# One yield more ahead of three readers, z loaded once, and a warm-up in half rows: a three-layer kernel on one Trainium2 core

## The chip, the cores and the metric

The kernel runs on one core of a Trainium2 chip. The core has five engines that run their own instruction queues and wait for one another through semaphores: TensorE (PE, matrix products; PEld is its weight load), VectorE (DVE), ScalarE (ACT), GpSimd (POOL) and SyncE (SP). SP, ACT and POOL also issue DMA transfers. The metric is the device time of one execution in microseconds.

## The reference

Two batches of 3136 tokens with 256 features pass through three layers:

```python
scores = (1 / S) * z @ z.T                    # attention, z has 64 features
x = u * (np.maximum(scores, 0) ** 2 @ v)
u1 = x + (x.T @ U @ V).T                      # layer 1: rank-32 token mixing
x = u1 + np.maximum(u1 @ w_ch1, 0) @ w_ch2    # 256 -> 1024 -> 256
u2 = x + real(fft(fft(x, axis=1), axis=2))    # layer 2: Fourier mixing
un = (u2 - mean) / sqrt(var + 1e-6)           # over the features
out = u2 + np.maximum(un @ w_ch1b, 0) @ w_ch2b
```

## The kernel before

**Number format.** Products run in a single-pass float32 format. Each operand is split into a rounded part and a remainder (a cast on ACT in `hcopy`, line 93, and a subtraction on DVE in `sub`, line 96), and a product is the sum of three (high by high, high by low, low by high).

**Attention** (lines 385 to 751) goes by batch, by 7 query chunks of 448 tokens and by 13 pairs of 128 keys. For z the two parts lie on top of each other in one tile of 128 partitions, T1 (high in the lower 64, remainder in the upper 64), and T2 holds them the other way round, so that two products with K = 128 give the scores. `load_z` (395) brings a chunk of z in twice, once for each half of the partitions, `split_z` (401) makes T1 and, for the very first chunk, T2. Lines 659 to 672 are the start of the program: three products of a zeroed tile, then the first loads and splits. The first loads are the only ones that also use ACT's DMA queue.

**Layers 1 and 2** go by 28 chunks of 448 tokens: 14 of layer 1, 14 of layer 2. The order of work is written by hand, from line 980. A chunk has 8 steps; at step k PE makes hidden block k (`hidden`, line 324, six products into one of three psH buffers, then `Hh` on ACT and `Hl` on DVE) and the six products of `project` (339) for the hidden block of two steps before, into psC, which has one buffer for each half of the output. After the last of them `finish` (360) reads psC on DVE; in layer 2 it multiplies by `rs`, one over the standard deviation, spread over 128 partitions (line 377, and 371 in the last chunk), adds x (379) and stores.

Between these products each step advances a list of Python generators by one `yield`; newer ones of the next chunk stand first. What a generator issues up to its next `yield` comes, on every engine, behind the products of that step. Three kinds matter here:

- `prep2` (274) of each layer-2 chunk starts at step 2 of the chunk before. It makes the mean (product of line 284), the centred and split input, the squares, their sum over the features (product of line 302 at step k=1 of the chunk itself), then a row of variances that goes through a small tile by DMA (`vv`, 306), a square root (310), a reciprocal chain (313 to 317), a DMA to DRAM (`rsd`, 319) and a broadcast back (`rs`, 321). The last three stand in step k=5.
- `fourier(b)` (782) adds the Fourier mixing of one batch to x, the first batch during layer 1, the second from step 106, the third step of the first layer-2 chunk. Its `fold` (792, six small additions on DVE) feeds `tokens` (810, transposes on PE) one step later; then come products along one axis (`axis49`), reloads, products along the other (`axis64`, 866), and `features` (887), nine products on PE, then DVE's additions to x. A single feature, number 128, is made apart (`feature128`, 881) and enters `features` as a row that two DMAs on POOL's queue write (line 953), read by the product of line 894.
- `weights`, `prep1` and the conversions, which the change doesn't touch.

POOL's queue holds `vv`, `rsd`, `rs`, the feature row and the reloads of T2, each issued in program order; an issue whose data isn't there yet holds up those behind it.

Of the kernel before, what the change touches and what calls it, by code (L numbers as in the profile page):

```python
# [10 lines left out]
F32 = mybir.dt.float32  # L11
# [10 lines left out]
CH = 448  # L22
# [55 lines left out]
def f(ap):  # L78
    return ap.bitcast(F32)
# [3 lines left out]
def program(ctx, tc, zT, v, uT, U, V, w1a, w2a, w1b, w2b, b49, f64, fd, rep, mask, out):  # L83
# [8 lines left out]
    def hcopy(o, i):  # L92
        nc.scalar.copy(o, i)  # L93

    def sub(o, a, b):
        tt(out=o, in0=a, in1=b, op=ALU.subtract)  # L96
# [10 lines left out]
    def ptile():  # L107
        return ctile("P", bufs=4)
# [114 lines left out]
    class Chunk:  # L223
# [4 lines left out]
        def load(self, a):  # L228
            self.a = a
            load(out=a, in_=aT_d[self.b][:, :, self.sl].rearrange("a p n -> p a n"))  # L230
            self.vr = com.tile([128, CH], F32, tag="Vr", name="Vr", bufs=1)
            for k in range(4):
                load(out=self.vr[k * 32 : k * 32 + 32, :], in_=V_d[:, self.sl])
# [40 lines left out]
        def prep2(self):  # L274
            b, mp = self.b, late["mp"]
            x = late["xT"][b][:, :, self.sl]
            h, l = c2(ctile("h", F32R)), c2(ctile("l", F32R))
            s = self.halved(x)
            yield
            st = self.stacked(*s)  # L280
            yield
            yield
            mu = misc()
            mm(mu[:, 0:CH], ones, st, start=True, stop=True)
            cc, sq = c2(ptile()), c2(ptile())
            for k in range(2):
                sub(cc[:, k], x[:, k], mu[:, 0:CH])
            yield
            for k in range(2):
                hcopy(h[:, k], x[:, k])  # L290
                sub(l[:, k], x[:, k], f(h[:, k]))
            self.x, self.h, self.l = x, h, l
            yield
            for k in range(2):
                act(out=sq[:, k], in_=cc[:, k], func=AF.Square)
            s = self.halved(sq)
            yield
            st = self.stacked(*s)
            yield

            ps = misc()
            mm(ps[0:1, 0:CH], ones[:, 0:1], st, start=True, stop=True)
            row = mp.tile([1, CH], F32, tag="vrow", name="vrow", bufs=1)
            hcopy(row, ps[0:1, 0:CH])
            vv, y, r0, ve = (mp.tile([112, 4], F32, tag=t, name=t) for t in ("vv", "vy", "vr", "ve"))
            late_dma(out=vv, in_=row.rearrange("o (p j) -> o p j", j=4))
            yield
            yield
            yield
            act(out=y, in_=vv, func=AF.Sqrt, bias=maskc[0:112, 3:4])  # L310
            nc.vector.tensor_scalar_add(ve, vv, 1e-6)
            yield
            nc.vector.reciprocal(r0, y)
            tt(out=y, in0=r0, in1=r0, op=ALU.mult)
            tt(out=y, in0=y, in1=ve, op=ALU.mult)
            nc.vector.tensor_scalar(out=y, in0=y, scalar1=-0.5, scalar2=1.5, op0=ALU.mult, op1=ALU.add)
            tt(out=y, in0=y, in1=r0, op=ALU.mult)
            row_d = rs_d[b * NC + self.c]
            late_dma(out=row_d.rearrange("(p j) -> p j", j=4), in_=y)
            self.rs = mp.tile([128, CH], F32, tag="rs", name="rs")  # L320
            late_dma(out=self.rs, in_=row_d.partition_broadcast(128))
            yield
# [62 lines left out]
    def attention(stack):  # L385
# [7 lines left out]
        Uhl = att.tile([128, 25, 2, RANK], F32R, tag="U", name="Uhl", bufs=1)  # L393

        def load_z(b, c):
            raw = att.tile([128, CH], F32, tag="zraw", name="zraw")
            for h, dma in enumerate((load, nc.scalar.dma_start if (b, c) == (0, 0) else load)):
                dma(out=raw[h * 64 : h * 64 + 64, :], in_=zT[b, :, c * CH : c * CH + CH])
            zraw[b, c] = raw

        def split_z(b, c):
            raw = zraw.pop((b, c))
            if c == 0:
                T1[b] = big.tile([128, S], F32R, tag="T1", name=f"T1_{b}")
            dst = T1[b][:, c * CH : c * CH + CH]
            hcopy(dst, raw)
            if (b, c) == (0, 0):
                t = T2[0, 0] = att.tile([128, CH], F32R, tag="T2", name="T2")
                hcopy(t[64:128], raw[64:128])
                sub(dst[64:128], raw[64:128], f(dst[64:128]))  # L410
                sub(t[0:64], raw[0:64], f(dst[0:64]))
            else:
                sub(dst[64:128], raw[64:128], f(dst[64:128]))
            if c == NC - 1:
                T1d[b] = att.tile([128, 2, 64], F32R, tag="T1d", name=f"T1d_{b}")
                for h in range(2):
                    nc.vector.tensor_copy(T1d[b][:, h, :], f(T1[b][:, S - 64 : S]))
# [238 lines left out]
        jobs = conversions()  # L656


        t = ptile()
        nc.vector.memset(t[:, 0:352], 0.0)  # L660
        hcopy(t[:, CH : CH + 8], t[:, 0:8])
        ps = pmg.tile([128, 512], F32, tag="g", name="ps_g")
        for k in range(3):
            mm(ps[:, 0:352], t[:, 0:128], t[:, 0:352], start=True, stop=True)
        load_z(0, 0)
        load_v(0, 0)
        load_z(0, 1)
        load_v(0, 1)
        split_z(0, 0)
# [112 lines left out]
    def fourier(b):  # L782
# [64 lines left out]
        for i in range(10):  # L847
            if i < 8:
                fold(i)
            if 0 < i < 9:  # L850
                tokens(i - 1)
            if i == 7:
                load(out=raw128[0:32, :], in_=xT[b][0:1, 1, :].rearrange("o (s p) -> o s p", p=98))
            if i > 1:
                axis49(i - 2)
            yield
# [82 lines left out]
        for pairs in (range(0, 3), range(3, 6), range(6, 9), range(9, 13)):  # L939
            first = 2 * pairs[0]  # L940
            k = min(2 * pairs[-1] + 2, KPOS) - first
            Th, Tl = (mp.tile([128, 2, CH], F32R, tag=t, name=t, bufs=1) for t in ("Th", "Tl"))
            for g in pairs:
                axis64(g, first, Th, Tl)
                if g + 3 < 13:
                    fetch(g + 3)
                if g == 1:
                    feature128()
                if g == pairs[-1]:

                    row = rows[pairs[0] // 3 % 2]
                    for j, x in enumerate((ch, cl)):
                        nc.gpsimd.dma_start(
                            out=row[j : j + 1, 0 : k * 64].rearrange("o (k n) -> o k n", n=64),
                            in_=x[first : first + k, :],
                        )
                if late_adds is not None and next(late_adds, "end") == "end":
                    late_adds = None
                yield
            yield  # L960
            late_adds = features(first, k * 64, Th, Tl, row)
            next(late_adds)
            yield
# [94 lines left out]
```

## Time and profile before

| | us |
|---|---|
| three runs: median (lowest, highest) | 1218.28 (1218.10, 1219.21) |
| the profiled execution | 1218.11 |
| its span, first to last instruction | 1216.3 |
| PE busy | 1202.9 |
| DVE busy | 829.8 |
| ACT busy | 652.5 |
| POOL busy | 46.8 |
| share of PE in the chain that ended last | 90% |

The span is what the profiler saw from the first instruction to the last; the profiled execution's time has 1.8 us around it. Busy times are unions, with matmuls shown longer than their distance, so PE can be called busy across short waits. A wait is read from the idle time in front of an instruction and from what ended it; the loss is read from the distance of starts.

### The profile page before, as it was taken

Reading aid. Unit: us, or ns where it says so; the run is one execution under the profiler, and the core shown is the slowest. Engines: PE = TensorE matmul, PEld = TensorE weight load, DVE = VectorE, ACT = ScalarE, POOL = GpSimd, SP = SyncE. Lnnn points to the kernel's source line nnn. Section 1 sums busy time; section 2 is a strip of 40 time slices with the busy share of each in tenths; the row PEclk is TensorE's granted clock in tenths of the full one; section 3 lists DMA queues with packets and bytes.
Section 4 is the critical chain, followed back from the end, with each engine's and each line's share of the span. In section 5 each row is a group of like instructions: output and inputs, shape, how many; then the busy total and the mean of one; then the engine's idle time right before and its main releaser. Section 6 shows DMA issues by size and latency. Waiting matters only on the chain.

```text
span 1216.3 us, 16363 instructions
## 1 busy us (share of the span) xinstructions
PE 1202.9 (99%) x6038; PEld 1102.4 (91%) x6038; DVE 829.8 (68%) x1565; ACT 652.5 (54%) x1052; POOL 46.8 (4%) x94
## 2 busy tenths in 40 slices
PE   9999999999999999999999999999999999999998
PEld 7999999999999999999899998999989889999997
DVE  7867777888666667666555456476576688666664
ACT  7767667777666566665433334333255444444442
POOL 0000000000000000000000000000000101000100
PEclk9999999999999999999999999999999999999999
DMA  5302220333122012211111102212012111111111
GB/s 153 104 22 69 68 64 26 117 93 105 44 64 64 9 57 77 60 40 54 38 51 53 46 23 85 81 45 62 5 57 73 48 39 31 39 31 38 31 39 46
DMA packets 58688, 68.56 MB, mean 56 GB/s; under 512 B 11630, under 2 KB 53712, under 8 KB 58608
## 3 DMA queue, kind: packets, MB, share of 16 engines
q1 hardware_dynamic: 54144, 61.13, 16.4%
q0 software_dynamic: 4384, 6.27, 2.6%
q8 instruction: 47, 0.77, 0.3%
q14 instruction: 33, 0.27, 0.1%
q10 hardware_dynamic: 80, 0.11, 0.0%
HBM read 44.86 MB, written 19.56 MB: 53 GB/s over the span
## 4 chain that ended last, share of the span: by engine, by line
PE 90%; DVE 4%; issue 3%; DMA 1%; ACT 1%; POOL 0%; SPq 0%; DVEq 0%; POOLq 0%; ACTq 0%
PE psO L574 12%; PE psO L571 12%; PE psO L573 11%; PE psH L330 6%; PE psH L329 6%; PE psH L331 6%; PE psC L355 6%; PE psC L354 6%; PE psC L356 6%; PE psS L542 6%; PE psS L541 6%; PE ps_g L628 1%; PE ps_m L607 1%; DVE Hl L335 1%; DVE l L96 0%
## 5 line engine op out<-in xcount | busy, mean ns | idle before, releaser
L571 PE MATMUL psO<-h,Vt 128*128 128x448 f32 x700 | 256.6, 367 | 0.1
L574 PE MATMUL psO<-h,Vt 128*128 128x448 f32 x700 | 256.5, 366 | 0.0
L573 PE MATMUL psO<-l,Vt 128*128 128x448 f32 x672 | 246.3, 367 | 0.3 <-DVE l L96 0.2
L547 ACT ACTIVATE P<-psS 128x896 f32<-128x896 f32 (+1 forms) x183 | 161.6, 884 | 147.7 <-PE psS L542 147.2
L335 DVE SCALAR_TENSOR_TENSOR Hl<-psH,Hh 128x448 fp32r<-128x448 f32 x224 | 139.6, 623 | 142.7 <-ACT Hh L334 141.6
L334 ACT ACTIVATE Hh<-psH 128x448 fp32r<-128x448 f32 x224 | 121.8, 544 | 200.2 <-PE psH L331 197.1
L96 DVE TENSOR_TENSOR l<-P,h 128x896 fp32r<-128x896 f32 (+1 forms) x197 | 201.2, 1021 | 23.5 <-ACT h L93 17.7
L551 DVE CAST h<-P 128x896 fp32r<-128x896 f32 (+1 forms) x183 | 111.0, 606 | 145.7 <-ACT P L550 144.6
L550 ACT ACTIVATE P<-P 128x896 f32<-128x896 f32 (+1 forms) x183 | 168.4, 921 | 5.7
L329 PE MATMUL psH<-h,w 128*128 128x448 f32 x448 | 167.9, 375 | 0.0
L330 PE MATMUL psH<-l,w 128*128 128x448 f32 x448 | 164.5, 367 | 0.2 <-DVE l L96 0.2
L331 PE MATMUL psH<-h,w 128*128 128x448 f32 x448 | 164.5, 367 | 0.0
L355 PE MATMUL psC<-Hl,w 128*128 128x448 f32 x448 | 163.7, 365 | 0.0
L354 PE MATMUL psC<-Hh,w 128*128 128x448 f32 x448 | 163.7, 365 | 0.0
L356 PE MATMUL psC<-Hh,w 128*128 128x448 f32 x448 | 163.2, 364 | 0.0
L571 PEld LDWEIGHTS psO<-h,Vt 128*128 128x128 f32 x700 | 131.6, 188 | 11.4 <-DVE aT L586 0.6
L574 PEld LDWEIGHTS psO<-h,Vt 128*128 128x128 f32 x700 | 131.6, 188 | 11.2 <-DVE Vt L96 0.3
L573 PEld LDWEIGHTS psO<-l,Vt 128*128 128x128 f32 x672 | 126.4, 188 | 11.3 <-DVE l L96 0.9
L541 PE MATMUL psS<-T 128*128 128x448 f32 x336 | 125.2, 373 | 0.8 <-DVE T L96 0.8
L542 PE MATMUL psS<-T,T 128*128 128x448 f32 x336 | 124.2, 370 | 0.0
L329 PEld LDWEIGHTS psH<-h,w 128*128 128x128 f32 x448 | 84.7, 189 | 7.9 <-ACT h L93 0.3
L331 PEld LDWEIGHTS psH<-h,w 128*128 128x128 f32 x448 | 84.4, 188 | 7.3
(276 smaller groups left out, 1421.8 us busy)
## 6 DMA issues: line engine op xcount, KB each, us to landing
uT<-in_uT SPq DMA_DIRECT2D x14, 448.0 KB, 4.2
vraw<-in_v SPq DMA_DIRECT2D x24, 256.0 KB, 2.7
out<-P SPq DMA_DIRECT2D x27, 224.0 KB, 2.0
aTd<-aT SPq DMA_DIRECT2D x13, 448.0 KB, 3.0
P<-aTd SPq DMA_DIRECT2D x13, 448.0 KB, 3.6
scr<-wst SPq DMA_DIRECT2D x16, 256.0 KB, 2.0
Vr<-Vd SPq DMA_DIRECT2D x56, 56.0 KB, 3.0
rs<-rsd POOLq DMA_DIRECT2D x14, 224.0 KB, 3.6
```

The source lines that it names most:

```text
L96: tt(out=o, in0=a, in1=b, op=ALU.subtract)
L329: mm(ps[:, 0:CH], wh, self.h[:, a], start=a == 0, stop=False)
L330: mm(ps[:, 0:CH], wh, self.l[:, a], start=False, stop=False)
L331: mm(ps[:, 0:CH], wl, self.h[:, a], start=False, stop=a == 1)
L354: mm(dst, wh, h, start=k == 0, stop=False)
L355: mm(dst, wh, l, start=False, stop=False)
L356: mm(dst, wl, h, start=False, stop=k == 7)
L541: mm(ps[:, j, 0:CH], k, q1, start=True, stop=False)
L542: mm(ps[:, j, 0:CH], k, q2, start=False, stop=True)
L571: mm(dst, vh, hj, start=p == 0 and j == 0, stop=False)
L573: mm(dst, vh, lj, start=False, stop=False)
L574: mm(dst, vl, hj, start=False, stop=p == 12)
```

## The change

- **Sum product and `rs`:** one more `yield` in `prep2` between the split squares and the product of line 302, and one more between the issues of `rsd` and `rs`.
- **z:** `load_z` loads 64 partitions once; `split_z` casts them into the lower half of T1 and writes the remainder, by a subtraction that reads the lower half, into the upper. T2 of the first chunk is made from the same 64 partitions.
- **Warm-up:** the zeroed tile gets a place of its own; the first loads are issued ahead of the products; one product over all rows stays, and eight in the single-pass format over the lower or the upper 64 rows follow, by turns into two PSUM banks.
- **Fold:** a `yield` in `fourier` after fold 0.
- **Feature row:** its DMAs are issued with the first axis product of a group of pairs (with pair 1 in the first group) and no longer with the last.

```diff
@@ prep2
             st = self.stacked(*s)
             yield
+            yield
 
             ps = misc()
             mm(ps[0:1, 0:CH], ones[:, 0:1], st, start=True, stop=True)
...
             late_dma(out=row_d.rearrange("(p j) -> p j", j=4), in_=y)
+            yield
             self.rs = mp.tile([128, CH], F32, tag="rs", name="rs")
             late_dma(out=self.rs, in_=row_d.partition_broadcast(128))
@@ load_z, split_z
-            raw = att.tile([128, CH], F32, tag="zraw", name="zraw")
-            for h, dma in enumerate((load, nc.scalar.dma_start if (b, c) == (0, 0) else load)):
-                dma(out=raw[h * 64 : h * 64 + 64, :], in_=zT[b, :, c * CH : c * CH + CH])
+            raw = att.tile([64, CH], F32, tag="zraw", name="zraw")
+            load(out=raw, in_=zT[b, :, c * CH : c * CH + CH])
...
-            hcopy(dst, raw)
+            hcopy(dst[0:64], raw)
+            sub(dst[64:128], raw, f(dst[0:64]))
             if (b, c) == (0, 0):
                 t = T2[0, 0] = att.tile([128, CH], F32R, tag="T2", name="T2")
-                hcopy(t[64:128], raw[64:128])
-                sub(dst[64:128], raw[64:128], f(dst[64:128]))
-                sub(t[0:64], raw[0:64], f(dst[0:64]))
-            else:
-                sub(dst[64:128], raw[64:128], f(dst[64:128]))
+                hcopy(t[64:128], raw)
+                sub(t[0:64], raw, f(dst[0:64]))
@@ attention, start
-        t = ptile()
-        nc.vector.memset(t[:, 0:352], 0.0)
-        hcopy(t[:, CH : CH + 8], t[:, 0:8])
-        ps = pmg.tile([128, 512], F32, tag="g", name="ps_g")
-        for k in range(3):
-            mm(ps[:, 0:352], t[:, 0:128], t[:, 0:352], start=True, stop=True)
+        t = att.tile([128, 360], F32R, tag="warm", name="warm", bufs=1)
+        nc.vector.memset(f(t[:, 0:352]), 0.0)
         load_z(0, 0)
         load_v(0, 0)
+        hcopy(t[:, 352:360], f(t[:, 0:8]))
+        ps = [pmg.tile([128, 512], F32, tag=g, name="ps_" + g) for g in "gm"]
+        mm(ps[0][:, 0:352], f(t[:, 0:128]), f(t[:, 0:352]), start=True, stop=True)
+        for k in range(8):
+            p = slice(k % 2 * 64, k % 2 * 64 + 64)
+            w = t[p, 0:352]
+            mm(ps[k % 2][:, 0:352], w[:, 0:128], w, start=True, stop=True)
@@ fourier
                 tokens(i - 1)
+            if i == 0:
+                yield
             if i == 7:
...
-                if g == pairs[-1]:
+                if g == max(1, pairs[0]):
 
                     row = rows[pairs[0] // 3 % 2]
                     for j, x in enumerate((ch, cl)):
-                        nc.gpsimd.dma_start(
+                        late_dma(
```

`late_dma` is another name for `nc.gpsimd.dma_start` (line 90).

## Rows read from the trace of the kernel before

**Rows 1.** The page, busy us (share of the span) and instructions of each engine
```profile
PE 1202.9 (99%) x6038; PEld 1102.4 (91%) x6038; DVE 829.8 (68%) x1565; ACT 652.5 (54%) x1052; POOL 46.8 (4%) x94
```

**Rows 2.** Waits of PE: line <- releaser: us in total, times, longest
```profile
PE ps_x L894 <- DMA row<-ecl: 2.6, 1, 2.6
PE ps_m L302 <- DVE sm L96: 1.9, 2, 1.5
...
PE ps_g L814 <- DVE y L803: 0.4, 1, 0.4
PE ps_x L814 <- DVE y L803: 0.2, 1, 0.2
```

**Rows 3.** Timeline of the start: start, us, engine, line, operation, count [idle before]
```profile
0.74 0.60 SPq L398 DMA_DIRECT2D zraw<-in_zT  x1
...
4.74 1.15 ACT L93 CAST T<-zraw 128x448 fp32r<-128x448 f32 x2 [2.51 <-DMA zraw<-in_zT]
...
6.01 0.74 PE L541 MATMUL psS<-T 128*128 128x448 f32 x1 [0.84 <-DVE T L96]
...
9.13 0.58 PE L542 MATMUL psS<-T,T 128*128 128x448 f32 x1
...
14.97 0.19 PEld L574 LDWEIGHTS psO<-h,Vt 128*128 128x128 f32 x1 [0.32 <-DVE Vt L96]
```

**Rows 4.** DMA issues within the first us: count, KB, us to landing
```profile
zraw<-in_zT SPq DMA_DIRECT2D x1, 112.0 KB, 2.6
```

**Rows 5.** Timeline of POOL's queue near 950 us, columns as above
```profile
951.36 0.58 POOL L321 DMA_DIRECT2D rs<-rsd  x1 [1.40 <-DMA rsd<-vy]
...
952.45 0.51 POOL L953 DMA_DIRECT2D row<-ecl  x1
```

**Rows 6.** Windows: stretch, its us, busy PE, PEld, DVE, ACT, POOL, PEclk, DMA
```profile
955.10:958.50 3.40, 3.02 (x9) 2.97 (x10) 0.65 (x2) 1.06 (x2) 0.00 (x0) 0.50 0.02 5
```

**Rows 7.** Timelines of DVE, POOL and PE in a steady layer-2 chunk, columns as above
```profile
1184.94 0.17 DVE L313 RECIPROCAL vr<-vy 112x4 f32<-112x4 f32 x1
...
1186.36 1.15 DVE L96 TENSOR_TENSOR l<-xT,h 128x448 fp32r<-128x448 f32 x2
...
1188.41 0.58 POOL L321 DMA_DIRECT2D rs<-rsd  x1 [1.67 <-DMA rsd<-vy]
...
1193.40 0.37 PE L302 MATMUL ps_g<-sm,ones 128*1 128x448 f32 x1
1193.70 1.15 DVE L377 TENSOR_TENSOR P<-psC,rs 128x448 f32<-128x448 f32 x2
1194.83 0.37 PE L354 MATMUL psC<-Hh,w 128*128 128x448 f32 x1
```

**Rows 8.** Line 321 from 1060 to 1200 us, seven issues: time to landing
```profile
DMA to landing us min/median/max: 3.3/3.6/3.7
```

**Rows 9.** Timelines of DVE, PE and POOL in the third and fifth chunk
```profile
977.17 0.62 DVE L906 SCALAR_TENSOR_TENSOR sm<-ps_m,maskc,A 128x384 f32<-128x384 f32 x1
...
981.75 0.42 DVE L96 TENSOR_TENSOR Tl<-ps_x,Th 128x256 fp32r<-128x256 f32 x1
...
988.88 0.36 PE L302 MATMUL ps_m<-sm,ones 128*1 128x448 f32 x1 [1.52 <-DVE sm L96]
989.09 0.68 PE L872 MATMUL ps_x<-f64s,wr 128*128 128x128 f32 x4
989.40 1.15 DVE L377 TENSOR_TENSOR P<-psC,rs 128x448 f32<-128x448 f32 x2
...
1030.82 0.58 POOL L321 DMA_DIRECT2D rs<-rsd  x1 [1.67 <-DMA rsd<-vy]
...
1035.02 1.15 DVE L377 TENSOR_TENSOR P<-psC,rs 128x448 f32<-128x448 f32 x2
```

**Rows 10.** Timeline of DVE at the end of the program
```profile
1203.44 0.17 DVE L313 RECIPROCAL vr<-vy 112x4 f32<-112x4 f32 x1
...
1210.36 0.63 DVE L371 TENSOR_TENSOR P<-psC,rs 128x448 f32<-128x448 f32 x1 [1.97 <-DMA rs<-rsd]
```

## The prediction, made before the changed kernel was seen

> **What bounds the kernel now.** I read the busy times first. TensorE (PE) is busy 99% of the span [rows 1], so only two things can move the end: moments in which PE waits, and the stretches before its first and after its last useful product. The other engines matter only through the wait that they end. The second view is the list of PE's waits; it names the feature row's DMA, the sum product of line 302, and the fold [rows 2]. An idle time there is less than the loss: products of 448 columns start 0.20 us apart and are shown for 0.36, so each wait costs its idle time plus 0.16. From the list I went to the timeline around each wait, to the start [rows 3, 4], and to the last transfer that somebody waits for, `rs`: the final product on VectorE (DVE) stands idle for it until 1210.36 us [rows 10]. The third thing to see is what has little room but waits for nothing yet. That is the middle of a steady second-layer chunk [rows 7].
>
> **Start.** Line 398 loads z twice; the first cast waits for the ACT queue's copy, and the first score product stands at 6.01 [rows 3]. The SP copy was issued at 0.74 and landed 2.6 us later, at 3.34 [rows 3, 4]. With that copy alone, cast, subtraction and score product follow as before: 4.74 - (3.34 + 0.08, the delay from landing to cast) = 1.3 us earlier. The subtraction now reads 64 partitions and writes the other 64, as line 271 does already; its length in time is that of its 448 columns, so it costs the same. PE still waits for DVE at 14.97 [rows 3], so the gain carries on only if that chain moves along. Gain between 0 (v, whose load is issued at the same time as before, sets the pace) and 1.3; I take 1.3, what the z rows themselves give. The warm-up becomes one whole product and eight half ones. The clock is low through 9.13, where a product is shown with 0.58 instead of 0.36 [rows 3]; whether it rises sooner no row tells. As DVE leads there, I take nothing for it, between 1.0 lost and 1.0 won (five products by 0.2). The other 27 SP copies become half as many; nobody on PE waited for them, so nothing.
>
> **Fold.** Only fold 0 gets a step more; folds 1 to 7 keep their distance but move off the step in which DVE also has the chunk's norm halves. Both waits, 0.4 + 0.2 + 2 x 0.16 = 0.9 us, go [rows 2]. The same step in the first batch moves nothing that waited. Gain 0.9 (bounds 0.4 and 1.0).
>
> **Feature row.** PE stood 2.6 us at line 894 [rows 2], because the row's two DMAs sat on POOL's queue behind `rsd` and `rs` of a chunk and went out last at 952.45 [rows 5]. Then the granted clock was 0.50, that is 1.2 of 2.4 GHz, for 3.40 us of which PE was busy 3.02 [rows 6]. Work that took 3.02 at half rate takes 1.5. Issued with the first of its pairs (with pair 1 in the first group), the row lands steps ahead. What is queued behind it on POOL is the next `vv` or `rsd`, two issues of 0.5 us later at most, with several us to spare. Gain 2.6 + 0.16 + 1.5 = 4.2.
>
> **Sum product.** Line 302 moves from step k=1 to k=2 of the next chunk. Its two waits go: 1.9 + 2 x 0.16 = 2.2 [rows 2]. But everything issued behind it in the generator moves too: the copy to `vrow`, `vv`, the square root, the reciprocal chain, `rsd`, `rs`. The first three have steps of room. The last has not, and the second new yield can't help it: `rsd` and `rs` stand in this order on POOL either way, and `rs` waits for the landing of `rsd`.
>
> **What the later `rs` costs, steady chunk.** Before: reciprocal at 1184.94, `rs` issued at 1188.41 [rows 7], landing 3.3 to 3.7 later [rows 8], say 1191.9, so 6.97 us after the reciprocal. Its reader, line 377, starts at 1193.70: 1.8 us of room. After: the reciprocal comes a step later, behind that step's `Hl` and the two `l` subtractions of the next chunk, which start at 1186.36 and 0.53 apart. That puts it at 1187.4 or a little sooner, since the old chain no longer stands ahead of them: 2.4 us later. `rs` lands at 1194.3, line 377 starts at 1194.4, 0.7 late. Queued behind it on DVE are line 379 and the next `Hl`, which have two steps. But its first product also frees the single buffer psC: it ends at 1195.0. PE wants to write there at line 354, at 1194.83 before, and 0.20 sooner after, as line 302 no longer stands ahead of that step: 1194.63. PE waits 0.42 us. No row of before shows this wait. Bounds by the landing's spread: 0.2 to 0.6; zero if the chain took 0.4 us less. Ten chunks stand like this one (the first, fourth and sixth to thirteenth of the second layer): 10 x 0.42 = 4.2 (2 to 6).
>
> **The chunks between.** The fourier stage loads DVE in four chunks. In the second, PE has the feature products between, so nothing. In the third, line 302's 1.52 us wait [rows 9] hid that line 377 was late as well: it starts at 989.40, 0.5 after line 302. Now the feature step and its six late additions come a step later in the chunk. From the first DVE instruction of the features, 977.17, to line 377 it was 12.23 us; the two `l` (1.07), one `Hl` (0.53) and one `Tl` (0.42) leave that stretch, 10.2 remain. From the end of the feature products PE needs three steps of 2.43 (twelve products), two groups of axis products (0.5 each, 989.09 and on) and six hidden products (1.22) to reach line 354: 9.5. DVE begins 0.3 to 0.85 behind PE, takes 10.2, and 0.63 + 0.05 for the first product: 11.2 to 11.7. PE waits 1.7 to 2.2 [rows 9]; I take 2.1, as the reciprocal chain stands ahead of the features. In the fifth chunk `rs` was issued at 1030.82 and landed 3.4 later, 0.8 before line 377 [rows 9]; a shift of 2.4 with the same corrections (+0.08 + 0.05 + 0.20 - 0.3) gives 1.6, and the features that come a step later some more: 1.8 (1.2 to 2.2).
>
> **End.** The last chunk's reciprocal goes from 1203.44 behind the next `Hl`, a step, 2.44 us. `rs` and the final products are a chain with no room: line 371 already waits for `rs` [rows 10]. Loss 2.44; bounds 2.3 and 2.6.
>
> **Sum**, against the profiled execution of 1218.11 us (span 1216.3 and 1.8 around it; the median of the runs is 1218.28, 0.17 more): 1218.11 - 1.3 - 0.9 - 4.2 - 2.2 + 4.2 + 2.1 + 1.8 + 2.44 = 1220.05, so **1220.0**. The waits that the change names are worth 8.6 us; what it moves late costs 10.5. A difference of 0.2%, 2.4 us, is about what a measurement of this kernel can tell from no change; 1220.0 lies inside it. Its own range is 1217.5 to 1222.5.
>
> **Rivals.**
> (a) Faster: the late `rs` doesn't reach PE in steady chunks, because the chain from reciprocal to landing takes under 6.4 us instead of 6.97, or `Hl` and `l` run sooner. Then 4.2 and about 1 of the fifth chunk's 1.8 fall away: 1214.8. Against it: seven landings with a spread of 0.4. For it: the whole wait hangs on 0.4 us per chunk. 0.20.
> (b) Slower: the new waits of about 2 us in the third and fifth chunk pull the clock down. 2.6 us of idle did [rows 2, 6], 1.52 us did not [rows 9]; the point lies between. Each costs what the row's cost, 1.5: 1221.5 with one, 1223.0 with both. 0.25 in all.
> (c) The change doesn't do what it says: the first score product isn't earlier, because v or the first weight of the loads sets it, or fold 1 still waits. Then 1.3 + 0.5 are missing: 1221.8. 0.08.
> (d) Faster still: `rs` lands 1.1 us sooner than the 3.5 taken above. The steady waits go as in (a), and the end loses 1.3 instead of 2.4: 1213.7. The rows show 3.3 to 3.7 in seven of seven [rows 8]: 0.03. A rule of the Trainium skill would have it so: DMA: Bandwidth & Descriptors (Anatomy of one DMA, SWDGE path) prices such a transfer at about 2.0 us and its bytes over 436 GB/s, for 224 KB an estimate of 2.5 us; by that rule the sum is 1213.7, and the trace disagrees.
> The forecast itself: 0.44.
>
> **How the numbers follow.** Faster by over 0.2% (under 1215.8): most of (a) and (d), 0.20. Slower by over 0.2% (over 1220.7): nearly all of (b) and (c) and the upper third of the forecast, but a part of each falls back under the bound: 0.37. Within: 0.43. The range from 1214.5 to 1223.0 takes in (a), one or both of (b), and the bounds of the unknown costs (2 to 6 for the steady chunks, 1.0 either way for the clock at the start).
>
> **What would show it.** Right: no wait at lines 894, 302 and 814; in the list of PE's waits line 354 waiting for DVE line 377, ten times or more, some 0.2 to 0.3 us idle each and once near 2; line 377 on DVE waiting for the DMA `rs`; line 371 at the end waiting over 4 us instead of 1.97; the first score product near 4.7. Wrong: line 377 starting on PE's heels (then (a)); a stretch of clock 0.50 after 950 us (then (b)); a first score product later than 5.5 (then (c)).

## The result, and the profile of the changed kernel

The changed kernel takes 1229.04 us (median of four executions, 1228.94 to 1229.62), the kernel before 1218.19; the ratio is 1.0088, with a 95% interval from 1.0071 to 1.0106. It is 10.9 us slower. The forecast was 1220.0, and its range ended at 1223.0.

The busy times come first. The span grew by 11.5 us, but PE is busy only 5.3 us more than in [rows 1], so about half of the loss is idle time of PE:

```profile
span 1227.9 us, 16353 instructions
...
PE 1208.2 (98%) x6042; PEld 1101.4 (90%) x6042; DVE 830.5 (68%) x1565; ACT 650.0 (53%) x1052; POOL 47.1 (4%) x94
```

The list of PE's waits answers [rows 2], columns as there. Every wait that the change names is gone (lines 302, 814 and 894 of before are 303, 816 and 898 here, and none is listed). One line has taken their place:

```profile
PE psC L356 <- DVE P L379: 8.5, 11, 2.3
```

Line 356 is the first product of `project` (354 before), line 379 the read of psC times `rs` (377 before). The list of DVE's waits says what line 379 and the last chunk's line 373 (371 before) wait for:

```profile
DVE P L379 <- DMA rs<-rsd: 7.0, 12, 0.8
DVE P L373 <- DMA rs<-rsd: 4.9, 1, 4.9
```

The start answers [rows 3]: the timeline of PE shows the half products in pairs, side by side, and the first score product at 4.70 us instead of 6.01.

```profile
2.76 0.66 PE L668 MATMUL ps_g<-warm 64*128 64x352 f32 x1
2.76 0.66 PE L668 MATMUL ps_m<-warm 64*128 64x352 f32 x1
...
4.70 0.74 PE L540 MATMUL psS<-T 128*128 128x448 f32 x1 [0.40 <-DVE T L96]
```

The late `rs` in the third, fourth, fifth and thirteenth chunk of layer 2 answers [rows 7, 9]. In these timelines of DVE and PE the brackets show two different things. At 1012.83 and 1202.00 line 379 itself waits for `rs`. At 986.22 it waits for nothing: DVE comes to it late, and PE stands 2.29 us.

```profile
986.22 1.15 DVE L379 TENSOR_TENSOR P<-psC,rs 128x448 f32<-128x448 f32 x2
986.98 0.44 PE L356 MATMUL psC<-Hh,w 128*128 128x448 f32 x1 [2.29 <-DVE P L379]
...
1012.83 1.16 DVE L379 TENSOR_TENSOR P<-psC,rs 128x448 f32<-128x448 f32 x2 [0.45 <-DMA rs<-rsd]
1013.60 0.45 PE L356 MATMUL psC<-Hh,w 128*128 128x448 f32 x1 [1.38 <-DVE P L379]
...
1037.40 0.44 PE L356 MATMUL psC<-Hh,w 128*128 128x448 f32 x1 [1.86 <-DVE P L379]
...
1202.00 1.16 DVE L379 TENSOR_TENSOR P<-psC,rs 128x448 f32<-128x448 f32 x2 [0.53 <-DMA rs<-rsd]
1202.77 0.44 PE L356 MATMUL psC<-Hh,w 128*128 128x448 f32 x1 [0.30 <-DVE P L379]
```

Right behind the two longest of them the granted clock falls to 0.50, 1.2 of 2.4 GHz, as it did once in [rows 6]. The windows view (columns as there):

```profile
987.61:991.02 3.41, 3.41 (x13) 2.89 (x12) 2.22 (x5) 1.10 (x3) 0.00 (x0) 0.50 0.48 157
1038.81:1042.22 3.41, 3.41 (x11) 3.07 (x10) 1.30 (x4) 1.53 (x3) 0.54 (x1) 0.50 0.37 135
```

The end answers [rows 10]; these are timelines of DVE and POOL:

```profile
1214.11 0.17 DVE L314 RECIPROCAL vr<-vy 112x4 f32<-112x4 f32 x1
...
1217.93 0.58 POOL L323 DMA_DIRECT2D rs<-rsd  x1 [2.03 <-DMA rsd<-vy]
...
1221.55 0.62 DVE L373 TENSOR_TENSOR P<-psC,rs 128x448 f32<-128x448 f32 x1 [4.93 <-DMA rs<-rsd]
```

One more row is one that nobody had looked for. Line 216 is a product at the beginning of layer 1. The first row is the kernel before's, the second the changed kernel's:

```profile
632.59 0.70 PE L216 MATMUL ps_m<-wst,repc 128*128 128x256 f32 x2
...
634.25 0.71 PE L216 MATMUL ps_m<-wst,repc 128*128 128x256 f32 x2
```

The 1.3 us won at the start have become 1.66 lost. Attention took 3.0 us longer, with no wait and no product more. The products simply start further apart: worked out from the start times, in stretches of 15 us, products of 448 columns stand 202.6 ns apart in the kernel before (with two slow stretches of 206.7, near 115 to 185 and 505 to 565 us), and 204.2 to 205.2 ns everywhere in the changed one. In layer 1 both have 205.6, in layer 2 both 202.7, where nothing of the fourier stage stands between.

The granted clock differs too. In this profile it is 0.95 of 2.4 GHz from 7.98 us on, in the kernel before 1.00; the windows view has the same stretch of both, the kernel before first:

```profile
60.00:105.00 45.00, 45.00 (x228) 41.62 (x227) 32.03 (x63) 30.27 (x45) 1.02 (x2) 1.00 0.17 47
...
60.00:105.00 45.00, 45.00 (x227) 41.23 (x226) 31.78 (x61) 30.35 (x43) 1.02 (x2) 0.95 0.17 47
```

It is not what attention lost by. Three of the versions below have the same warm-up and a clock of 1.00 in attention (the sum product's step undone, the reciprocal put back, the step at `rs` undone). Their products start 204.8 ns apart as well, and their line 216 stands at 633.87 to 634.04. The changed kernel's three other executions, with a mean clock of 0.996, took 1228.94 to 1229.09 us.

Set side by side, the lag of the changed kernel grows like this (from the start times on PE; in a chunk, at the last product of `project` for hidden block 0, in the third chunk for block 4):

| at (us of before) | what | lag (us) |
|---|---|---|
| 6.01 | first score product | -1.3 |
| 632.59 | line 216, attention is over | +1.7 |
| 938.07 | layer 2, second chunk | +0.8 |
| 978.81 | third chunk, past the feature row; here nine feature products (1.6 us) are still to come in the changed kernel | -5.5 |
| 1036.95 | sixth chunk, behind the wait at 1037.40 | +1.5 |
| 1056.81 | seventh chunk | +3.8 |
| 1195.83 | last chunk | +8.0 |
| 1210.40 | last product | +8.2 |
| 1216.3 | end of span | +11.5 |

### The profile page after: what moved, and what is told of

Same layout as the page of the kernel before. It is cut to its first block, busy times and chain, and to the rows that moved or that the text cites. A ratio compares the mean times of both kernels' runs of the same rounds, so it can differ in the third digit from the quotient of the medians.

```text
span 1227.9 us, 16353 instructions
## 1 busy us (share of the span) xinstructions
PE 1208.2 (98%) x6042; PEld 1101.4 (90%) x6042; DVE 830.5 (68%) x1565; ACT 650.0 (53%) x1052; POOL 47.1 (4%) x94
## 4 chain that ended last, share of the span: by engine, by line
PE 83%; issue 7%; DVE 5%; DMA 4%; ACT 1%; POOL 1%; DVEq 0%; POOLq 0%; ACTq 0%
PE psO L570 12%; PE psO L573 12%; PE psO L572 11%; PE psS L540 6%; PE psS L541 6%; PE psC L356 5%; PE psH L331 5%; PE psH L332 5%; PE psH L333 5%; PE psC L357 5%; PE psC L358 5%; DMA rs<-rsd 3%; PE ps_g L627 1%; PE ps_m L606 1%; DVE P L379 1%
## 5 line engine op out<-in xcount | busy, mean ns | idle before, releaser
L336 ACT ACTIVATE Hh<-psH 128x448 fp32r<-128x448 f32 x224 | 121.6, 543 | 202.6 <-PE psH L333 200.0
L356 PEld LDWEIGHTS psC<-Hh,w 128*128 128x128 f32 x448 | 84.3, 188 | 20.1 <-issue 8.4
L331 PEld LDWEIGHTS psH<-h,w 128*128 128x128 f32 x448 | 84.7, 189 | 8.1 <-ACT h L93 0.3
```

The source lines that it names most:

```text
L331: mm(ps[:, 0:CH], wh, self.h[:, a], start=a == 0, stop=False)
L356: mm(dst, wh, h, start=k == 0, stop=False)
```

## The experiments

Line numbers shift by a few between the kernels below; line 302/303 is the sum product, 354 to 356 the first product of `project`, 377 to 379 the read with `rs`. The kernel before was run beside each group, with medians from 1217.4 to 1219.2 us; ratios are to it. The theories at stake: A, the later reciprocal chain makes the loss; B, features that come a step later keep DVE late in the third chunk; C, the loss lies in the attention stage, and then D to G, by what.

### The step ahead of the sum product

**Undone in the changed kernel:**

```diff
             st = self.stacked(*s)
             yield
-            yield
 
             ps = misc()
```

> The changed kernel without the step ahead of the sum product; all other parts stay. Theory A (the later reciprocal chain is the loss): line 356 no longer waits, so of the changed kernel's 1229.0 us go its stalls at that line (10.5 us of lengthened starts in all, the steady ones 4.3 of them), the two stretches of low clock (2.8) and what the end grew by (3.3), and the two waits of the sum product (2.2) come back: 1214.6 us. Theory B (features that come a step later keep DVE late in the third chunk, whatever rs does): the 2.5 us stall and its low clock stay: 1218.4. Theory C (the loss lies in the attention stage and at the start): 1225 or more. In attention the products should keep the changed kernel's distance of starts, 204.8 ns, if that distance belongs to the program, and may take another if it changes from execution to execution.

Measured: 1216.24 us, ratio 0.9985 (0.9976 to 0.9994). The waits at line 356 are gone and the wait at the end is back at 1.8 us, so A holds: this one step made a kernel that is a little faster than before into one 0.9% slower. It falls 1.6 us short of A's figure of 1214.6, in the direction of B, and PE's waits say where: the sum product waits longer than in [rows 2], at 984.26 us 2.0 (1.52 before, [rows 9]) and at 1010.78 0.8 us, and after the first the clock fell once. Attention kept 204.8 ns: the distance belongs to the program.

```profile
PE ps_g L302 <- DVE sm L96: 2.8, 2, 2.0
```

**Alone in the kernel before:**

```diff
             st = self.stacked(*s)
+            yield
             yield
 
             ps = misc()
```

> The kernel before with the one step ahead of the sum product and nothing else. Theory A: the two waits of the sum product go (2.2 gained), the steady stalls (4.3), the longer end (3.3) and a stall of about 2 us in the third and in the fifth chunk come, with or without 1.4 us of low clock each: 1218.2 - 2.2 + 4.3 + 3.3 + 4 = 1227.6, or up to 1230.4 with the clock. Theory C: no more than 1220. The attention stage is that of the kernel before, so its distance of starts should be 202.6 ns with two stretches of 206.7 near 115 to 185 and 505 to 565 us, if that pattern belongs to the program.

Measured: 1225.78 us, ratio 1.0069 (1.0054 to 1.0084), 8.4 us slower; C is out as the main cause. A's figure was 1227.6. The two lists of waits show the changed kernel's picture without its other parts:

```profile
PE psC L355 <- DVE P L378: 7.5, 12, 1.7
...
DVE P L378 <- DMA rs<-rsd: 7.3, 10, 1.7
...
DVE P L372 <- DMA rs<-rsd: 4.4, 1, 4.4
```

It also shows no wait at the feature row, though the row's DMAs weren't moved: with the norm chain a step later, they went out at 945.88 and 946.40, ahead of `rsd` (953.16) instead of behind `rs` as in [rows 5]. Attention has the kernel before's pattern, but for one stretch near 325 us.

**The reciprocal put back, the sum product left late:**

```diff
             late_dma(out=vv, in_=row.rearrange("o (p j) -> o p j", j=4))
             yield
             yield
-            yield
             act(out=y, in_=vv, func=AF.Sqrt, bias=maskc[0:112, 3:4])
```

> The changed kernel with one of the three steps taken out between the issue of vv and the square root: the sum product stays late, but square root, reciprocal chain, rsd and rs stand in their old steps again. Theory A: the stalls of line 356, their low clock and the longer end go, and the sum product's waits do not come back: 1229.0 - 10.5 - 2.8 - 3.3 = 1212.4. Rival (vv hasn't landed when its reader comes, so ACT or DVE waits and passes it on to PE): vv is issued in one step and read two steps of 2.4 us later, its landing takes 2 to 3 us and the cast ahead of it waits too; then new waits stand at the square root and some of the gain is missing, 1215 to 1220. Theory B: the third chunk's stall stays, 1216.2.

Measured: 1217.06 us, ratio 0.9993 (0.9983 to 1.0002). All steady waits and the longer end are gone (line 372 waits 1.9 us at the end, as in [rows 10]), so they hang on the place of the reciprocal chain and not on the sum product. No new wait stands at the square root. What stays of the waits of PE is mostly one, in the third chunk, where line 378 waits for no DMA:

```profile
PE psC L355 <- DVE P L378: 2.7, 3, 1.9
```

That is B, and the time lies near B's figure.

**The step between `rsd` and `rs` undone in the changed kernel:**

```diff
             late_dma(out=row_d.rearrange("(p j) -> p j", j=4), in_=y)
-            yield
             self.rs = mp.tile([128, CH], F32, tag="rs", name="rs")
```

> The changed kernel without the step between rsd and rs. As the prediction has it, rs waits on POOL's queue for the landing of rsd, 1.7 us, which is under a step, so where its issue stands among the other engines' steps changes nothing: 1229.0, within 0.5. Rival: the later place of rs in POOL's order puts other POOL issues ahead of it, and a part of the stalls at line 356 is due to that: 1225 to 1228.

Measured: 1229.76 us, ratio 1.0088 (1.0071 to 1.0105), the changed kernel's own ratio, to within the 3 us that the two intervals leave. The changed kernel's trace says more: all 14 issues of `rs` waited 1.4 to 2.1 us for `rsd` to land, so the step ahead of them held up nothing, as predicted. In its profile one `rsd` landed late (`rs` waited 3.39 us for it on POOL's queue, 1.67 in [rows 7]), PE waited 2.2 us in the sixth chunk, and the clock fell there and not behind the fifth chunk's 1.9 us: at that length it does not fall every time.

### The step after fold 0 and the feature row

**The feature row's DMAs sooner, alone in the kernel before:**

```diff
-                if g == pairs[-1]:
+                if g == max(1, pairs[0]):
```

> The kernel before with the feature row's DMAs at the first axis product of a group, nothing else. Prediction's term: the wait of 2.6 us, its 0.16 of lengthened start and the 1.5 of low clock go: 1217.4 - 4.2 = 1213.2 us. Rival: the sum products' waits after it (0.5 and 1.5 us) grow as PE now comes sooner to DVE's late work, so that only 2 to 3 us are won: 1214.4 to 1215.4. The low clock at the row's wait need not have come in every execution, so the median may gain 1.5 us less.

Measured: 1214.91 us, ratio 0.9973 (0.9962 to 0.9985), 3.4 us faster. The row's wait and the low clock behind it are gone; the smaller of the sum product's two waits grew from 0.3 to 1.1 us, which is the rival, and the time lies in its range.

```profile
PE ps_m L302 <- DVE sm L96: 2.6, 2, 1.5
```

**The step after fold 0, alone in the kernel before:**

```diff
                 tokens(i - 1)
+            if i == 0:
+                yield
             if i == 7:
```

> The kernel before with the step after fold 0 alone. The prediction's term: the two folds' waits go, 0.9 gained, 1217.4 beside a kernel before of 1218.3. Theory B (features a step later push DVE's work towards the sum products): the sum product of the third chunk waits 2.0 us instead of 1.5 and the fourth chunk's 0.8 to 1.0, as in the changed kernel without the sum's step, so 1.3 come back, and in executions in which the clock falls at the 2.0 us, 1.4 more: 1218.7 to 1220.

Measured: 1214.72 us (1213.69 to 1217.92), ratio 0.9973 (0.9963 to 0.9983), 4.0 us faster: neither figure. B's part is there: the sum product of the third chunk waits 2.0 us, that of the fourth 0.8, and in the profiled execution the clock fell after the first. But the row's wait is gone too. In the timelines of POOL and PE its second DMA goes out only half a us sooner than in [rows 5], behind `rs` as before, but the product that reads it comes at 957.05, where PE had come to it at 952.92 in the kernel before (it started at 955.48 after 2.56 idle), and finds it landed:

```profile
951.90 0.52 POOL L955 DMA_DIRECT2D row<-ecl  x1
...
957.05 0.34 PE L896 MATMUL ps_g<-row,fN 128*128 128x384 f32 x1
```

So two parts of the change remove the same 4 us, and the prediction counted it with one and the folds' 0.9 us on top.

### What attention lost

**The new warm-up alone in the kernel before** (the lines of the warm-up in the diff above, z loaded twice as before):

> The kernel before with the new warm-up alone (own place for the zeroed tile, loads first, one whole product and eight of 64 rows by turns); z is still loaded twice. For the 3.0 us that the attention stage lost: theory D (the warm-up, by its tile's place or its other number of products, sets the pattern in which later products start): distance of starts 204.8 ns through attention as in the changed kernel, 1218.2 + 3.0 and up to 1 less for a sooner clock: 1220.2 to 1221.2. Theory E (the split of z sets it): 202.6 with the two slow stretches, 1217.2 to 1218.2. The clock's rise should come sooner than the 9.6 us of the kernel before if it hangs on the half products alone, and at the same time as there if it needs the first score product.

Measured: 1219.89 us, ratio 1.0020 (1.0010 to 1.0029), 204.2 to 205.1 ns a start. It is the warm-up, which issues nothing after 5 us. The clock rose at 10.87 us, later than the 9.60 of the kernel before, so the half products alone did not bring it sooner. The next pair takes it apart.

**Its products, but the zeroed tile in its old place among the P buffers:**

```diff
-        t = att.tile([128, 360], F32R, tag="warm", name="warm", bufs=1)
+        t = ctile("P", bufs=4)[:, 0:360].bitcast(F32R)
```

> The kernel before with the new warm-up (loads first, one whole product and eight of 64 rows), but with the zeroed tile in its old place among the P buffers. The new warm-up in its own tile took the attention products from 202.6 to 204.7 ns a start. Theory F (where the tile lies, which moves what is placed after it and the turn of the P buffers, sets the pattern): 202.6 ns with the two slow stretches of 206.7, layer 1 as early as before, about 1217.4 us beside the 1217.4 of the kernel before. Theory G (the number or kind of the products ahead sets it): 204.7 ns and 1219.9 as with the own tile.

**Its place, but the three whole products and the order of before:**

```diff
-        t = ptile()
+        t = att.tile([128, 360], F32, tag="warm", name="warm", bufs=1)
         nc.vector.memset(t[:, 0:352], 0.0)
-        hcopy(t[:, CH : CH + 8], t[:, 0:8])
+        hcopy(t[:, 352:360], t[:, 0:8])
```

> The kernel before with its three whole warm-up products and its order of issue, but with the zeroed tile in a place of its own. The other half of the pair: by theory F 204.7 ns a start in attention, 2.9 us lost there from 15 to 600 us, 1220.3 us; by theory G 202.6 ns and 1217.4 us. If neither kernel of the pair shows 204.7, place and products are needed together.

Measured: 1218.15 us, ratio 0.9998 (0.9989 to 1.0008), with the products; 1220.88, ratio 1.0021 (1.0011 to 1.0031), with the place; line 216 stands at 632.79 and 635.84. Theory F, the place. A tile that no instruction touches after the first microseconds slows products for 600 us.

**A spare tile in the kernel before, warm-up untouched,** of 360, 512, 384 and 368 columns:

```diff
         t = ptile()
+        spare = att.tile([128, 360], F32, tag="warm", name="warm", bufs=1)
+        nc.vector.memset(spare[:, 0:8], 0.0)
         nc.vector.memset(t[:, 0:352], 0.0)
```

> The kernel before, its warm-up untouched, with one more tile of 128 x 360 float32 (1440 bytes in each partition) in the pool of the attention stage, of which 8 columns are zeroed and which nobody reads. Theory F1 (the tile's bytes move what lies behind them, and that sets the distance of starts): 204.7 ns through attention, 2.4 to 3 us lost by 600 us, 1220 to 1221 us. Theory F2 (not the bytes, but that the zeroed tile no longer takes a turn of the P buffers): 202.6 ns with the two slow stretches, as before, 1217.5 to 1218.3 us.

> The same with a spare tile of 512 columns, 2048 bytes in each partition. Theory F1a (it is the remainder of the shift that counts, so that a shift by a power of two changes nothing): 202.6 ns with the two slow stretches. Theory F1b (any shift does it): 204.7 ns or a third pattern. Theory F2: as before.

> The kernel before with a spare tile of 384 columns, 1536 bytes in each partition, a multiple of 512. If the remainder to 512 bytes or less decides: 202.6 ns a start with two slow stretches, as before, 1217.5 to 1218.7 us. If only multiples of 1024 or 2048 are harmless: 204.7 ns or a third pattern, 1220 to 1221 us.

> The same with 368 columns, 1472 bytes, a multiple of 64 and not of 128. If the remainder to 64 bytes decides (1440 leaves 32): as before, 1217.5 to 1218.7 us. If a remainder to 128 or more decides: 204.7 ns or a third pattern, 1220 to 1221 us.

The rows of line 216, for 360 columns, then 512, then 368 (each from its kernel's timeline of PE; 632.59 in the kernel before):

```profile
635.60 0.70 PE L216 MATMUL ps_m<-wst,repc 128*128 128x256 f32 x2
```

```profile
633.19 0.70 PE L216 MATMUL ps_m<-wst,repc 128*128 128x256 f32 x2
```

```profile
626.43 0.70 PE L216 MATMUL ps_m<-wst,repc 128*128 128x256 f32 x2
```

| spare bytes in each partition | distance of starts in attention (ns) | line 216 at (us) | ratio (95%) |
|---|---|---|---|
| none | 202.6, slow stretches of 206.7 | 632.59 | 1 |
| 1440 (odd times 32) | 204.2 to 205.2 | 635.60 | 1.0019 (1.0009 to 1.0028) |
| 2048 | 202.6 and 206.7, as with none | 633.19 | 1.0000 (0.9990 to 1.0009) |
| 1536 (odd times 512) | 202.6 and longer stretches of 206.7 | 634.71 | 0.9995 (0.9986 to 1.0005) |
| 1472 (odd times 64) | 200.9 to 202.0 | 626.43 | 0.9947 (0.9932 to 0.9962) |

It is the bytes, not the turn of the P buffers (F1 and not F2). Multiples of 512 left the two levels as they were, 1440 gave a third level, and 1472 a fourth that is faster than the kernel before: 1212.09 us, 0.5% won by a tile that nobody reads. That was among nobody's expectations. All seven kernels here with 1440 bytes more in the attention stage's pool show the third level, and none of the other thirteen does. Which tile matters, and by what mechanism, stays open.

**The changed kernel with its own tile made 512 wide:**

```diff
-        t = att.tile([128, 360], F32R, tag="warm", name="warm", bufs=1)
+        t = att.tile([128, 512], F32R, tag="warm", name="warm", bufs=1)
```

> The changed kernel with the zeroed tile of the warm-up made 512 columns wide (2048 bytes in each partition) instead of 360; 352 are used as before. If the place of what lies behind it is what the attention stage lost by, the distance of starts there goes from 204.8 to 202.6 ns with two slow stretches of 206.7, and 3.0 us go: 1229.0 - 3.0 = 1226.0 us. With longer slow stretches, as one kernel with z loaded once had, 1.2 come back: 1227.2. If place is not the cause in the changed kernel: 1229.0.

Measured: 1226.51 us, ratio 1.0062 (1.0047 to 1.0078); line 216 at 631.25, 3.0 us sooner than in the changed kernel and 2.6 sooner than in the same kernel with the step at `rs` undone, which like this one ran at a clock of 1.00. That confirms the term in the changed kernel itself.

**z loaded once, alone in the kernel before** (`load_z` and `split_z` of the diff above):

> The kernel before with z loaded once and spread on chip, nothing else. Prediction's term: first score product at 4.7 instead of 6.0 us, and all later work 1.3 sooner: 1217.0. Bounds: DVE's chain for v sets the pace through 15 us (no gain), or the three whole warm-up products, which end near 5.2, stand in front of the first score product: then it starts at 5.0 to 5.2 and 0.8 to 1.0 is won, 1217.4. A rival by the pattern: it gives the gain back in attention, 1218.3.

Measured: 1217.94 us, ratio 0.9995 (0.9986 to 1.0005). The interval takes in both no gain and the 1.3 us of the term. The trace decides for the rival: the first score product starts at 4.81, close to the 4.7 of the prediction, but line 216 stands at 633.02, so the gain was given back in attention. The stretches of 206.7 ns lie at 15 to 95, 205 to 265 and 505 to 565 us. That z moved them isn't shown: in the kernel with the fold's step alone, whose attention is that of the kernel before, they lie at 205 to 265 as well and not at 115 to 185. With one placement of the tiles the slow stretches can thus stand elsewhere without a change of attention.

### Versions made from the findings

**The changed kernel with the reciprocal put back, the fold's step taken out and the tile in its old place** (three of the diffs above together):

> The changed kernel with three edits: the step ahead of the square root taken out (1217.06 us with that alone), the step after fold 0 taken out, so that the features stand a step sooner, and the zeroed tile in its old place. Theory B (the 1.9 us stall of line 356 that the sooner reciprocal left in the third chunk comes from features a step late): it goes, with the low clock of 1.7 us that most executions showed; the folds' waits of 0.9 come back: 1217.06 - 2.1 - 1.7 + 0.9 = 1214.2. Theory F with it: 2.9 us less in attention: 1211.3. If theory B is wrong the stall stays: 1215.1 with F, 1218 without F.

Measured: 1215.31 us, ratio 0.9974 (0.9964 to 0.9984). PE's wait in the third chunk fell from 1.9 to 1.3 us, so B holds for a third of it; the rest stays, and attention had the early slow stretches of the kernel with z alone: line 216 stands at 632.34, 0.3 us ahead of the kernel before where the start had won 1.3.

**The kernel before with z loaded once, the half-row products in the old place, and the sooner feature row:**

> The kernel before with z loaded once, the half-row warm-up with its tile in the old place, and the sooner feature row; no step in the norm chain and none after the fold. Feature row alone gave 3.4 us over the kernel before (0.9973). The sooner start adds 1.3 if the attention pattern stays that of the kernel before: 1218.3 - 3.4 - 1.3 = 1213.6. Rival (the sooner start shifts where the slow stretches of 206.7 ns lie, as in the combined kernel, which had lost 1.3 again by 600 us): 1214.9.

Measured: 1213.92 us, ratio 0.9959 (0.9945 to 0.9974), as expected. Attention has nearly the slow stretches of before, and line 216 stands at 631.47.

**The same with the reciprocal a step sooner than in the kernel before** (the diff of the reciprocal above, on this kernel):

> The kernel before with z loaded once, the half-row warm-up in the old place and the sooner feature row (1213.9 us with these), and one of the three steps between vv and the square root taken out, so that the reciprocal chain, rsd and rs come a step of 2.44 us sooner than in the kernel before, the opposite of the change. At the end line 371 no longer waits its 1.97 us for rs; then the last product sets the end: between 1.0 and 2.0 us gained, 1212.0 to 1212.9. Nothing else should change, as nobody else waited for rs. Rival: the sooner chain of six small DVE instructions falls into the step that holds the next chunk's subtractions, and PE waits for those: 1213.9 or more.

Measured: 1212.53 us (1212.21 to 1213.20), ratio 0.9950 (0.9938 to 0.9963), faster than both kernels. The interval overlaps that of the version without it, so what this one step brings is read from the trace. At the end line 370 now waits for PE and no longer for `rs`, which was the last wait of [rows 10]:

```profile
1205.12 0.62 DVE L370 TENSOR_TENSOR P<-psC,rs 128x448 f32<-128x448 f32 x1 [1.21 <-PE psC L355]
```

## Why the prediction was wrong

The forecast was a loss of 2 us, too small to tell from none; the loss is 10.9 us: 1220.0 against 1229.0. The step that failed is the term of the warm-up, put at nothing; three other terms were too small. By the steps of the prediction:

**Right.** *Start*: 1.3 us predicted, 1.3 at the first score product. *Fold*, *Feature row* and *Sum product*: the waits they name are gone from the list. *What the later `rs` costs*: the chain of argument (a step later behind `Hl` and the two `l`, `rs` late, line 377 late, PE held at the single psC) is what the rows show, and putting back the reciprocal alone removed it in the steady chunks. In the thirteenth, from whose rows the 0.42 was worked out, PE stood 0.30 us for the 0.26 in it. That the second yield of the norm chain is worth nothing agrees with its experiment and with the waits of `rs` for `rsd`.

**Mis-sized: the waits at psC.** The prediction had 4.2 (ten chunks) + 2.1 (third) + 1.8 (fifth) = 8.1 us. Measured by the lengthened distance of starts (idle time and 0.16 each): the eight steady chunks from the sixth on 0.32 to 0.78, together 4.3, mean 0.53 for 0.42, the longest behind an `rs` that waited 2.12 us for `rsd`; the first chunk 0.2; the third 2.5; the fifth 2.0; and the fourth 1.5, which the prediction had put among the steady ones. In sum 10.5, that is 2.4 more. The fourth chunk's error has a place: there too features stand on DVE, and their six late additions (1002.17, 1.94 us) and the two `l` come ahead of the reciprocal (1005.63), so that its reader starts 7.2 us later while PE wants psC 6.4 us later; in the thirteenth chunk PE wants it 7.3 us after the reciprocal (1195.03).

**Mis-weighed: the clock.** Rival (b) came true in full. Both long waits (2.3 and 1.9 us idle) were followed by 3.41 us of granted clock 0.50, which lengthened the starts by 1.3 and 1.5 us. The price was right, the chance of 0.25 too low. It rested on a point between 1.52 and 2.6 us of idle time from which the clock falls, and the profiles show none: behind 1.9 us it fell here and in two versions it did not (the step at `rs` undone, the reciprocal put back), and behind the 2.66 to 2.76 us at the feature row it stayed at 1.00 in three (the warm-up alone, its place alone, the spare 1440 bytes). The length of the wait alone doesn't decide; what else does stays open. In the range it took the whole upper end, and nothing was left for another error.

**Not counted: the place of the warm-up's tile.** The step that failed is the sentence on the warm-up, "I take nothing for it, between 1.0 lost and 1.0 won". It weighed the products and the clock, and not that the tile "gets a place of its own". That put 1440 bytes more into the pool of the attention stage and cost 3.0 us there, shown by the tile alone, the products alone, a spare tile, and the changed kernel with its tile made 512 wide (1226.51 us). How the place sets the distance of starts stays open. Without this term the time would still lie near 1226, above the range.

**Mis-sized: the end.** 2.44 predicted, 3.3 measured (the lag grows from 8.2 to 11.5). The step of 2.44 is there; beside it `rs` waited 2.03 us on POOL's queue for `rsd` to land, where it had waited 1.46 in the kernel before, and from line 373 to the end it took 6.3 us for 6.0.

These make 2.4 + 2.8 + 3.0 + 0.9 = 9.1 us. The forecast was 9.0 below the median; against the profiled execution, from which the terms are read, it was 9.6 below (1229.62 and 1220.05), so half a us has no place. Apart from that, the terms of the gains were not as separate as the sum had them: the fold's step by itself removes the feature row's wait (4.0 us in all), the sooner row does too (3.4), and so, in another way, does the later norm chain. In the sum this was harmless, since each wait was credited once, but the single terms would have misled anyone who chose among the parts: the step of the sum product brings 2.2 us, removes the feature row's wait as well, and still makes the kernel 8.4 us slower.

## What to carry to other kernels

A step that is moved takes along everything that is issued behind it in its generator: before moving a reader later, follow the chain to its last reader and ask how much room *that* one has; here the room was at the sum product and the lack at `rs`, and the profitable move was the opposite one. Gains that rest on waits of one place (a row's DMA, the features, a sum product) share that place, so try each part alone before adding them up. After any change of a tile's size or place, compare the distance of starts in stretches that the change doesn't touch; where it differs, pad the tile and measure a few sizes.

## What the runs showed that was not expected

Products of the same shape, in the same order, at a granted clock of 1.00 and with no wait between them ran at 201.4, 202.6, 204.8 or 206.7 ns a start, depending on the bytes of an unused tile in their pool. Over the attention stage that is a spread of 9 us (626.43 to 635.60 at line 216). At a granted clock of 0.95, in the changed kernel's profile, the distance was 204.8 ns too, as at 1.00. The layers, whose tiles come later in other pools, kept 205.6 and 202.7 ns in all these kernels. A kernel with both the 1472 bytes and the best set of changes was not tried.

With the same three whole products at the start, the clock rose at very different times: 9.6 us in the kernel before, 5.35 with the feature row sooner, 10.65 with the fold's step, 4.35 with the 1472 bytes. At line 216 the second of these kernels led by only 0.2 us, which fits the prediction's view that DVE leads there; how much of it the slow stretches took is not known.
